# A new order of all engine and queue instructions in a sliding-window attention and MLP kernel

## The chip, the core and the metric

The kernel runs on one core of a Trainium2 chip. A core has five engines that work side by side, each with its own queue of instructions: PE (matrix products), DVE (elementwise work and reductions), ACT (activation functions and copies), POOL and SP (here almost only issuing of transfers). Every engine takes its instructions strictly in the order in which they were emitted, and an instruction that waits for another engine or for a transfer holds up all that stand behind it on its own engine. Transfers are carried out by 16 DMA engines; they are issued by POOL (transfers that change the type) and SP (stores and transposing transfers). The metric is the device time of one execution in microseconds (us), lower being better.

## The reference

q, k and v have 8 batches, 8 heads, 576 rows and 64 columns, all in 32 bits. Attention looks back over a window of 128 rows with a bias that falls linearly with distance; its output is laid out as 4,608 rows of 512, normalised, sent through a two-layer MLP with 2,048 hidden columns, and added back.

```python
scores = scale * np.matmul(q, k.transpose(0, 1, 3, 2))
rel = pos[:, None] - pos[None, :]
mask = (rel >= 0) & (rel < window)                      # window = 128
scores = np.where(mask, scores + bias[None], -1e9)      # bias = slope of the head * -|rel|
attn = np.exp(scores - np.max(scores, axis=-1, keepdims=True))
attn = attn / (np.sum(attn, axis=-1, keepdims=True) + 1e-09)
x = np.matmul(attn, v)                                  # then (8, 576, 512)
mu, var = mean(x), mean((x - mu) ** 2)                  # over the 512 columns
xn = (x - mu) / np.sqrt(var + 1e-06) * g_ln
out = x + np.maximum(xn @ w_ch1, 0.0) @ w_ch2           # 512 -> 2048 -> 512
```

## The kernel before

**Tiles.** The 4,608 rows are cut into 36 blocks of 128, numbered 0 to 35 in the order in which they are worked on. The blocks go through the MLP in 11 chunks: four of two blocks, then seven of four. Chunks 0 to 3 do the two products plainly; from chunk 4 (`SEVEN`) on the second product is done with seven instead of eight partial products, from chunk 8 (`BOTH`) on the first as well.

**The steps of a block i**, with the names that stand in the order and in the texts:

- `q`, `k`, `v`: loads that change 32 bits to 16 on the way, issued by POOL (L501). Blocks 0 and 1 are loaded uncast by SP instead (`qs`, `ks`, `v0`), and cast by ACT, DVE or POOL (`cT`, `cv`).
- `T` (PE transpose, L653 and L701) with its eviction `eT`/`ev` to the tile `qkt`; from block 9 on `QT`, a transposing transfer issued by SP (L716).
- `Z`: matmuls that put the bias into the scores' PSUM (L756; blocks 0 to 4). `S`: scores (L740). `exa`, `exb`: exponentials on ACT (L789), two halves. `mka`, `mkb`: masks on DVE (L797).
- `pva`, `pvb`: products with v, whose extra column gives the sums (L818). `rc`, `nm`: reciprocal and scaling on DVE (L835, L839).
- `mu`, `sq`, `ln`, `rs`, `xs`: the normalisation; `sq` (L866 on ACT, L868 on DVE) and `xs` (L878, L902 to L907) can be on either engine. `TX`/`xt`: transpose of the normalised block on PE with its eviction; from block 6 on `XT`, a transposing transfer by SP (L936).
- MLP: `A` first product (L1227) and `r` its relu (L1242 DVE, L1244 ACT); `B` second product (L1264) and `o` (L1272). In the seven-product form `Pa` to `Pg` (L1009) with `sa` to `sd`, `ra` to `rg` (L1021), and `Ua` to `Ug` (L1138) with `ca`, `ja`, `rja` and the like for the first product. `out`: stores by SP (L1081).
- `G`, `Gk`, `Gc`, `Gkc`: the normalisation's gain is spread over partitions once (L431, L445 on PE). `scaleW`, `sumW`, `sumT`: sums and scalings of weights for the seven products. `~n`: n small matmuls without use, issued to fill a wait of PE (L1305).
- `w`: the weights' loads (four of w1, four of w2), on POOL as well.

**Buffers that make a step wait.** `qk16` has 5 tiles (q and k of block n wait until block n-5 has been transposed, by `T` or `QT`), `vx` has 9, `qkt` 6 (`QT` of a block waits for the scores that read the tile last), `ot` (the tile that is stored) 3 and `xb` 4. POOL's loads take eight semaphores in turn, so a load also waits until the load eight places ahead of it has landed.

**What sets the order.** Every engine's order, the engine where there is a choice, and the PSUM bank are written out in the string `ORDER` (L119 to L212): words `name:engine`, where T is PE, A is ACT, V is DVE, G is POOL and S is SP, with the bank behind it; `.i` marks the issue of a transfer. `Plan.run` (L80 to L115) walks through the string, checks that each step's inputs and bank are there, and emits the steps in that order. The prices that `add` and `Choice` are given at build time play no part in it:

```python
def Choice(names, full):
    return dict(full)
...
            name, where = word.split(":")
            t, e, b = by[name].pop(0), self.ENGINES[where[0]], [int(x) for x in where[1:]]
            assert e in t.eng and all(ready(d) for d in t.deps), name
```

Of the kernel before, what the change touches and what calls it, by code (L numbers as in the profile page):

```python
# [127 lines left out]
A1.6:T1 r1.8:A ln1:A S4:T0 r1.6:A B1.0:T2 exb4:A k7.i:G A1.2:T3 B0.0:T0 r1.2:A pvb4:T1 B1.4:T2 q9.i:G mreg11:A rc1.4:V nm1.4:V exa4:A A1.12:T3
mreg31:A q8.i:G mreg10:A mreg01:A sumT0.0:V B0.4:T0 ln0:A r1.12:V rs0:A mreg00:A T5:T1 mreg30:A sumT0.1:V B0.8:T0 ev5:A v10.i:G sumT0.2:V B1.8:T2
mreg20:A k8.i:G mreg21:A S5:T0 mmixc:V B1.12:T2 exa5:A k9.i:G sumT1.0:V B0.12:T0 z1:V exb5:A k10.i:G sumT1.1:V o1.0:V B3.0:T3 dist1a:G q10.i:G o0.0:V  # L130
T6:T1 pva4:T2 B3.4:T3 ev6:V k11.i:G z2:V mka5:V S6:T0 v6.i:G B3.8:T3 exb6:A rc0.4:V mkb5:V q11.i:G T7:T0 nm0.4:V pva5:T1 mu4:V ev7:A k12.i:G B3.12:T3
xs4:V rc0.5:V rs1:A v7.i:G B2.0:T2 exa6:A nm0.5:V o3.0:V TX4:T0 q12.i:G sq4:A pvb5:T1 QT9.i:S sumT0.3:V T8:T3 xt4:A B2.4:T2 rc1.5:V k13.i:G nm1.5:V
ev8:A mkb6:V S7:T0 v8.i:G QT10.i:S B2.8:T2 mu5:V exa7:A mka6:V v8.i:G xs5:V exb7:A B2.12:T2 v9.i:G TX5:T0 mkb7:V S8:T0 xt5:A q13.i:G pva6:T1 o2.0:V
exb8:A pvb6:T3 A2.0:T0 v11.i:G rc0.6:V mka7:V A2.12:T2 nm0.6:V rc1.6:V QT11.i:S nm1.6:V A2.2:T1 r2.12:A mkb8:V r2.0:A A2.6:T3 mnewc:V exa8:A r2.2:V
pvb7:T2 pva7:T0 sq5:A mu6:V rc1.7:V r2.6:V S9:T0 QT12.i:S mka8:V A2.14:T1 exa9:A rc0.7:V nm1.7:V B4.0:T3 exb9:A nm0.7:V r2.14:V A2.4:T2 mu7:V xs6:V
S10:T0 q15.i:G r2.4:A xs7:V A2.10:T0 XT6.i:S exa10:A q15.i:G z3:V pva8:T1 mka9:V r2.10:A B4.4:T3 XT7.i:S k14.i:G exb10:A pvb8:T2 k15.i:G A2.8:T0
rc1.8:V rc0.8:V nm0.8:V q14.i:G S11:T0 nm1.8:V r2.8:A B5.0:T1 mkb9:V exb11:A mkb10:V QT13.i:S pva9:T2 B5.4:T1 ln2:A mka10:V exa11:A rc0.9:V pvb9:T0
k17.i:G B5.8:T1 rs2:A sq6:A rc1.9:V nm0.9:V mka11:V q16.i:G pva10:T2 sq7:A S12:T0 nm1.9:V B4.8:T3 v13.i:G exb12:A mu8:V mu9:V sq8:V B5.12:T1 k15.i:G
sq9:A rc0.10:V mkb11:V B4.12:T3 v12.i:G o5.0:V ln9:A rs9:A exa12:A A3.2:T0 xs8:V q17.i:G nm0.10:V XT8.i:S A3.0:T1 mka12:V r3.2:A k16.i:G xs9:A o4.0:V
A3.6:T2 QT14.i:S scaleW0:V r3.0:A pvb10:T0 pva11:T3 r3.6:A A3.14:T1 out1.0.i:S rc1.10:V S13:T0 nm1.10:V r3.14:A pvb11:T2 mu10:V exb13:A A3.10:T0  # L140
rc0.11:V rc1.11:V nm0.11:V nm1.11:V A3.4:T1 exa13:A sq10:V XT9.i:S B6.0:T3 r3.10:A mu11:V sq11:V r3.4:A out0.0.i:S A3.8:T2 mkb12:V ln11:A B7.0:T0
rs11:A xs10:A xs11:V B6.4:T3 scaleW1:V r3.8:A XT11.i:S ln3:A B7.4:T0 scaleW2:A XT10.i:S A3.12:T1 mka13:V mkb13:V pva13:T2 QT15.i:S k19.i:G B6.8:T3
r3.12:V scaleW3:A rc0.13:V sumT1.2:V S14:T0 q18.i:G pva12:T1 B7.8:T0 rc0.12:V v15.i:G QT16.i:S nm0.12:V B6.12:T3 nm0.13:V v17.i:G rs3:A exb14:A
pvb13:T1 pvb12:T2 k18.i:G exa14:A rc1.13:V B7.12:T0 o6.0:V QT17.i:S v14.i:G nm1.13:V A4.0:T3 sumT1.3:V v16.i:G A4.5:T1 rc1.12:V o7.0:V r4.0:A v15.i:G
mu13:V A4.8:T3 nm1.12:V sq13:A mu12:V q19.i:G mkb14:V out2.0.i:S S15:T0 r4.5:A A4.15:T0 out3.0.i:S exa15:A out5.0.i:S A4.6:T2 r4.15:V exb15:A mka14:V
A4.11:T1 sq12:V S16:T0 A4.1:T0 r4.11:V exa16:A r4.8:V A4.2:T1 exb16:A r4.1:V A4.3:T3 mka15:V r4.2:A QT18.i:S q22.i:G ln13:A mkb16:V A4.10:T0 r4.6:A
mkb15:V q20.i:G A4.9:T1 r4.10:A mka16:V rs13:A k20.i:G pva14:T2 r4.9:A A4.12:T0 rc0.14:V xs12:V r4.3:A k21.i:G pvb14:T1 XT12.i:S sa4.0:V S17:T0
v22.i:G A4.4:T3 exa17:A nm0.14:V out7.0.i:S rc1.14:V sc4.0:V q22.i:G A4.14:T2 r4.12:A nm1.14:V exb17:A q21.i:G mka17:V A4.13:T0 r4.4:A mkb17:V A4.7:T1
QT19.i:S r4.14:A r4.13:V pva15:T3 r4.7:A Pa4.00:T2 sb4.0:V out4.0.i:S xs13:A pvb15:T0 Pa4.01:T2 rc0.15:V rc1.15:V nm0.15:V Pb4.00:T1 nm1.15:V XT13.i:S
Pa4.10:T2 Pb4.01:T1 mu15:V sa4.1:V sq15:A Pa4.11:T2 mu14:V Pb4.10:T1 ra4.0:V sq14:A pva17:T3 Pb4.11:T1 sb4.1:V Pc4.00:T2 ln15:A rb4.0:V S18:T0 rs15:A  # L150
xs15:A Pc4.01:T2 xs14:V Pd4.00:T1 sc4.1:V XT14.i:S exb18:A Pc4.10:T2 rc0.17:V Pd4.01:T1 sd4.0:V exa18:A Pc4.11:T2 XT15.i:S nm0.17:V pva16:T0 rc4.0:V
Pd4.10:T1 pvb16:T3 sd4.1:V QT20.i:S Pd4.11:T1 q24.i:G S19:T0 Pe4.00:T2 rd4.0:V exb19:A k22.i:G Pe4.10:T2 mka18:V Pe4.01:T2 QT21.i:S exa19:A k22.i:G
rc0.16:V Pf4.00:T1 rc1.16:V nm0.16:V Pe4.11:T2 v19.i:G Pf4.10:T1 re4.0:V pvb17:T0 Pf4.11:T1 k24.i:G rc1.17:V nm1.16:V Pf4.01:T1 nm1.17:V Pg4.00:T2
v18.i:G mu16:V A5.13:T3 rf4.0:V sq16:A q23.i:G mu17:V mkb18:V A5.8:T0 sq17:A r5.13:V k23.i:G S20:T0 ln17:A A5.1:T1 v21.i:G A5.2:T3 r5.1:A v22.i:G
exa20:A A5.11:T1 v20.i:G r5.2:A Pg4.01:T2 mka20:V exb20:A Pg4.10:T2 r5.11:V QT24.i:S A5.3:T3 rs17:A r5.8:A mkb20:V k26.i:G pvb18:T1 Pg4.11:T2 r5.3:V
QT22.i:S q26.i:G S21:T0 rc1.18:V pva18:T0 nm1.18:V A5.5:T3 q25.i:G exa21:A rg4.0:V A5.0:T1 r5.5:V k25.i:G exb21:A xs16:V A5.10:T2 rc0.18:V mka19:V
A5.7:T3 r5.10:A mkb21:V A5.14:T2 r5.0:V r5.7:A mka21:V out9.0.i:S A5.6:T1 r5.14:A XT16.i:S mkb19:V xs17:A A5.9:T3 nm0.18:V r5.6:V out6.0.i:S pvb19:T2
pva19:T0 r5.9:V A5.12:T1 rc0.19:V mu18:V rc1.19:V QT23.i:S sq18:V A5.4:T3 r5.12:A nm1.19:V A5.15:T1 r5.4:A sa5.0:V Pa5.00:T2 nm0.19:V r5.15:A pvb20:T3
sc5.0:V XT17.i:S Pa5.01:T2 mu19:V Pb5.00:T0 rc1.20:V sq19:A nm1.20:V Pa5.10:T2 out8.0.i:S sb5.0:V pvb21:T1 out10.0.i:S Pb5.01:T0 ln19:A sa5.1:V
Pa5.11:T2 rs19:A QT25.i:S Pb5.10:T0 ra5.0:V xs19:A S22:T0 Pb5.11:T0 xs18:V exb22:A sb5.1:V Pc5.10:T2 XT19.i:S Pc5.00:T2 rb5.0:V exa22:A pva20:T3  # L160
Pc5.11:T2 XT18.i:S q28.i:G Pc5.01:T2 Pd5.00:T0 rc5.0:V k29.i:G S23:T0 QT26.i:S Pd5.01:T0 rc1.21:V exa23:A sd5.0:V k27.i:G Pe5.00:T2 sc5.1:V Pd5.10:T0
exb23:A v24.i:G Pe5.10:T2 nm1.21:V Pd5.11:T0 mkb22:V q29.i:G S24:T0 rd5.0:V Pe5.11:T2 q27.i:G Pe5.01:T2 rc0.20:V nm0.20:V Pf5.10:T0 sd5.1:V Pf5.00:T0
re5.0:V pva21:T1 dist1b:G v23.i:G A6.6:T3 mka22:V Pf5.11:T0 rc0.21:V dist2:G r6.6:A nm0.21:V Pf5.01:T0 k30.i:G exa24:A pva22:T3 mu21:V mkb23:V
# [1184 lines left out]
```

## Time and profile before

| | us |
|---|---|
| three runs | 299.85, 296.86, 299.59 |
| their median | 299.59 |
| the profiled execution | 299.22 |
| its span (first to last instruction) | 297.06 |
| outside the span | 2.16 |

TensorE's granted clock in the profiled execution is 0.998 of full speed. Times in a profile are counted from the span's start. Per cent behind an engine are its busy time over the span. PE is the matmuls, PEld the loading of their weights, which goes on beside them; the matmuls overlap one another, so a matmul's own duration is longer than the step from one start to the next. In a timeline a line is a run of like instructions: start, duration, engine, line of the kernel, operation, out<-in, shape, count, and in brackets the idle time before it with what ended it. In the chain of waits a line is start, duration and the work that the end of the program was waiting for at that moment.

| engine | busiest groups by line (busy us) |
|---|---|
| PE | A 89.9, P 45.5 and 30.5, B 31.2, pv 26.8 |
| ACT | exp 67.8, relu 37.7, sq 20.3, c* 19.5 |
| DVE | masks 30.1, nm 29.2, j* 23.9, relu 21.0, r* of P 19.6 |
| POOL | loads of q 32.6, k 32.8, v 30.7 (issuing) |

The queue of cast loads moves 17.70 MB and takes 91.8% of the span's DMA time as the packets' durations add up, the other transfers 21.77 MB and 42.5%. From issue to landing a cast load takes a median of 7.6 to 8.6 us, `QT` 8.7, `XT` 5.2, a store of 256 KB 3.5.

### The profile page before, as it was taken

What the parts mean: (1) busy time and instruction counts of PE and PEld (TensorE: products, weight loads), DVE (VectorE), ACT (ScalarE), POOL (GpSimd) and SP (SyncE); (2) the same over time, 40 slices, a digit from 0 to 9 for tenths busy, and PEclk for the clock granted to TensorE, in tenths of its full rate; (3) what the DMA queues carried; (4) which work ended last, traced back from release to release, by engine and by line L of the source; (5) the groups of instructions that cost most, each with busy time, mean ns of one, the idle gap of its engine ahead of it and who ended that gap; (6) DMA issues with size and microseconds to landing.
All of it is one profiled execution on the core that took longest, in us unless ns stands there. A gap on an engine that the chain in (4) does not pass through costs nothing.

```text
span 297.1 us, 8787 instructions
## 1 busy us (share of the span) xinstructions
PE 288.4 (97%) x3589; PEld 226.6 (76%) x3589; DVE 234.8 (79%) x623; ACT 201.1 (68%) x363; POOL 106.1 (36%) x139
## 2 busy tenths in 40 slices
PE   8889999999999999999999999799999999999995
...
GB/s 181 163 196 187 202 166 154 149 136 138 137 195 159 205 167 151 154 148 195 150 154 178 174 176 132 143 157 134 50 55 125 2 18 73 90 28 81 71 21 195
DMA packets 163787, 40.04 MB, mean 135 GB/s; under 512 B 154017, under 2 KB 159137, under 8 KB 163746
## 3 DMA queue, kind: packets, MB, share of 16 engines
q0 software_dynamic: 110000, 17.70, 91.8%
q1 hardware_dynamic: 53744, 21.77, 42.5%
...
q14 instruction: 13, 0.11, 0.1%
q10 hardware_dynamic: 2, 0.00, 0.0%
...
## 4 chain that ended last, share of the span: by engine, by line
PE 79%; DMA 15%; POOL 2%; issue 1%; SPq 1%; DVE 1%; POOLq 0%
PE fb L1009 25%; PE fb L1227 22%; PE u L1138 12%; PE fb L1264 10%; DMA vx<-in_v_dram 9%; PE fb L818 4%; PE sc L740 4%; DMA qkt<-qk 3%; DMA qk<-in_q_dram 2%; DMA ks<-in_k_dram 2%; POOL qk L501 1%; PE fb L701 1%; SPq L485 0%; PE fb L921 0%; PE sc L756 0%
## 5 line engine op out<-in xcount | busy, mean ns | idle before, releaser
L1227 PE MATMUL fb<-xt,w1sb 128*128 128x256 f16 (+1 forms) x512 | 89.9, 326 | 0.1
L789 ACT ACTIVATE probs<-sc 128x1024 f16<-128x1024 f32 (+1 forms) x72 | 67.8, 974 | 24.5 <-PE sc L740 18.4
L1227 PEld LDWEIGHTS <-w1sb 128*128 128x128 f16 x512 | 54.9, 114 | 24.7 <-issue 0.7
L1009 PEld LDWEIGHTS <-ht 128*128 128x128 f16 x560 | 53.1, 98 | 7.2
L1244 ACT ACTIVATE ht<-fb 128x512 f16<-128x512 f32 x65 | 37.7, 599 | 24.1 <-PE fb L1227 24.0
L501 POOL DMA_DIRECT2D qk<-in_q_dram x38 | 32.6, 862 | 49.1 <-DMA qkt<-qk 46.2
L1009 PE MATMUL fb<-w2sb,ht 128*128 128x256 f16 x336 | 45.5, 273 | 0.0
L501 POOL DMA_DIRECT2D qk<-in_k_dram x38 | 32.8, 870 | 25.4 <-DMA qkt<-qk 17.3
L797 DVE TENSOR_TENSOR probs<-probs,mreg 128x1024 f16<-128x1024 f16 (+1 forms) x46 | 30.1, 669 | 4.7 <-ACT probs L789 4.6
L501 POOL DMA_DIRECT2D vx<-in_v_dram x36 | 30.7, 867 | 6.2 <-DMA w2sb<-in_moe_w_ch_dram 1.5
L1264 PE MATMUL fb<-w2sb,ht 128*128 128x512 f16 x128 | 31.2, 379 | 0.0
L1009 PE MATMUL fb<-ks,ht 128*128 128x256 f16 x224 | 30.5, 273 | 0.0
L839 DVE SCALAR_TENSOR_TENSOR xb<-fb,rec 128x256 f16<-128x256 f32 x72 | 29.2, 417 | 0.7
L818 PEld LDWEIGHTS <-probs 128*128 128x128 f16 x544 | 23.9, 97 | 7.3 <-issue 2.2
L818 PE MATMUL fb<-vx,probs 128*128 128x65 f16 x496 | 26.8, 193 | 1.9 <-DMA vx<-in_v_dram 1.9
L1161 DVE TENSOR_TENSOR ht<-u,probs 128x512 f16<-128x512 f32 x36 | 23.9, 686 | 4.9 <-PE u L1138 1.9
L835 DVE RECIPROCAL rec<-fb 128x4 f32<-128x4 f32 x72 | 12.2, 177 | 18.4 <-PE fb L818 16.9
L1242 DVE TENSOR_SCALAR ht<-fb 128x512 f16<-128x512 f32 x31 | 21.0, 686 | 6.8 <-PE fb L1227 6.6
L1151 ACT ACTIVATE probs<-u 128x512 f32<-128x512 f32 x35 | 19.5, 596 | 9.4 <-PE u L1138 6.1
L1021 DVE TENSOR_TENSOR ot<-fb,xb 128x512 f32<-128x512 f32 (+1 forms) x31 | 19.6, 636 | 6.1 <-PE fb L1009 5.6
L866 ACT ACTIVATE squares<-xb,mean 128x512 f16<-128x512 f16 x28 | 20.3, 723 | 3.1 <-DVE mean L857 2.8
L1138 PEld LDWEIGHTS <-w1sb 128*128 128x128 f16 x192 | 21.1, 114 | 0.4
(119 smaller groups left out, 440.7 us busy)
## 6 DMA issues: line engine op xcount, KB each, us to landing
...
w2sb<-in_moe_w_ch_dram POOLq DMA_DIRECT2D x4, 512.0 KB, 10.9
...
```

What stands on the lines that cost most here:

```text
L501: nc.gpsimd.dma_start(out=dst(p0, n), in_=src[b, :, s0 : s0 + n, :].rearrange("h p d -> p h d"))
L789: nc.scalar.activation(out=o, in_=n_, func=AF.Exp, scale=inv_sqrt_d)
L797: en.tensor_tensor(out=pv, in0=pv, in1=mask[:, 2 * half : 2 * half + 2, :, lo:], op=ALU.mult)
L818: nc.tensor.matmul(pp[:, hh * (D + 1) : hh * (D + 1) + D + 1], probs[i][:, bank, slot, side * P : side * P + P], vx[i if side else before] ...
L839: nc.vector.scalar_tensor_tensor(out=xb[c][:, j, 256 * half : 256 * half + 256].rearrange("p (h d) -> p h d", d=D), in0=pp[:, :, 0:D], sca ...
L1009: nc.tensor.matmul(o, lhs(f, p), rhs(f), start=first and f == 0 and (p == 0 or key[0] != key[p]), stop=f == F2 - 1, skip_group_check=True)
L1138: nc.tensor.matmul(late[bank][:, FOURTH * f : FOURTH * f + FOURTH], w, rhs[kb], start=first and f == kb == 0, stop=kb == 1, skip_group_che ...
L1161: nc.vector.tensor_tensor(out=o, in0=late[bank][:, :].rearrange("p (f c) -> p f c", f=2), in1=other.rearrange("p (f c) -> p f c", f=2), op ...
L1227: nc.tensor.matmul(fb[b][:, n_ * x : n_ * x + n_], w1f[f // CB][:, kb, (f + x) % CB, :], xt[c][:, kb, 0:n_], start=(kb == x == 0), stop=(k ...
L1242: nc.vector.tensor_scalar(out=o, in0=src, scalar1=0.0, scalar2=None, op0=ALU.max)
L1244: nc.scalar.activation(out=o, in_=src, func=AF.Relu)
L1264: nc.tensor.matmul(pm[:, 0 : c1 - c0], ht[c][:, f, j * P : j * P + P], w2sb[f // CB][:, f % CB, c0:c1], start=(f == 0), stop=(f == NFB - 1),)
```

## The change

`ORDER` is replaced as a whole; the steps, their number and what each computes stay. Four things differ: the order of the steps on each of PE, ACT, DVE, POOL and SP; the PSUM banks; the engine of some steps (`sq` on ACT 28 before and 26 after, `xs` on ACT 18 and 14, the relu of the seven-product form `rja`, `rjb`, `rjc` on ACT 19 and 24, `r` on ACT 65 and 66, `scaleW` on ACT 2 and 3, `ev` on ACT 4 and 2, one cast of block 1 from POOL to DVE); and the filling matmuls, 59 before and 72 after. Two prices at build time change as well. The whole diff replaces 93 lines of the string by 93; shown are the start, the place of `q11`, the late loads with the transposes `QT28` to `QT34`, and the prices. In the late part the words ending in `.i:G`, read from left to right, are POOL's queue.

```diff
--- before.py
+++ after.py
@@ the start, down to A0.2 @@
-iden1:G qs0.0.i:S dist:G ks0.0.i:S dist00:G dist01:G qs1.0.i:S iden2:G sid6:V ks1.0.i:S sid2:V iden3:V sid4:V sid5:V sid7:V v0.i:S sid0:V sid3:V
-sid1:V ~35 Za0:T0 cT0.00:A g.i:A cT0.10:G w0.i:G T0.0:T0 k2.i:G Zb0:T0 eT0.00:A cT0.01:A cT0.11:G ~7 Sa0:T0 eT0.01:A q2.i:G ~5 T0.1:T1 exa0:A cv0:A
-v1.i:G eT0.10:V ~2 Za1:T0 eT0.11:A Sa1:T0 k3.i:G Sb0:T0 G:T2 exb0:A q3.i:G Zb1:T0 Gc:A v3.i:G Sb1:T0 exa1:A pva0:T0 pvb0:T1 v2.i:G Gk:T2 rc0.0:V
-rc1.0:V exb1:A nm1.0:V nm0.0:V w1.i:G mu0:V w3.i:G xs0:V ~10 T2:T1 w2.i:G Z2:T0 ev2:V pva1:T0 q5.i:G pvb1:T3 rc0.1:V S2:T0 rc1.1:V nm0.1:V exb2:A
-k4.i:G nm1.1:V T3:T1 exa2:A mu1:V TX0:T0 q4.i:G xs1:V Z3:T0 xt0:A ev3:V v4.i:G pvb2:T3 TX1:T0 pva2:T1 S3:T0 xt1:V q8.i:G rc1.2:V exa3:A nm1.2:V
-A0.2:T0 w4.i:G rc0.2:V sq0:V exb3:A A0.6:T3 dist1:G Gkc:V nm0.2:V sq1:A A0.4:T2 r0.2:V k8.i:G mu2:V pvb3:T1 xs2:V r0.4:A pva3:T0 Z4:T0 sq2:A rc1.3:V
+dist:G qs0.0.i:S dist00:G ks0.0.i:S iden1:G dist01:G qs1.0.i:S iden2:G sid6:V v0.i:S sid3:V sid7:V sid5:V sid2:V sid4:V sid1:V ks1.0.i:S sid0:V
+iden3:V ~31 Za0:T0 Zb0:T0 cT0.00:A g.i:A cT0.10:G v1.i:G T0.0:T0 cT0.01:A w3.i:G eT0.00:A q2.i:G ~10 Sa0:T0 G:T1 exa0:A k2.i:G cT0.11:V cv0:A eT0.01:A
+k3.i:G T0.1:T2 Za1:T0 eT0.10:V v2.i:G Sa1:T0 eT0.11:A Sb0:T0 exb0:A q3.i:G exa1:A ~8 Zb1:T0 w0.i:G pvb0:T0 pva0:T2 Sb1:T0 rc1.0:V rc0.0:V k4.i:G
+nm1.0:V exb1:A nm0.0:V q4.i:G mu0:V Gc:A ~13 pvb1:T0 pva1:T2 xs0:V v3.i:G rc0.1:V w2.i:G ~10 T2:T3 k5.i:G TX0:T1 ev2:V Z2:T0 rc1.1:V q5.i:G nm1.1:V
+S2:T0 Gk:T3 exb2:A nm0.1:V w1.i:G exa2:A mu1:V xs1:V T3:T0 xt0:A v4.i:G sq0:V sq1:A TX1:T2 Z3:T0 xt1:V w4.i:G ev3:V pvb2:T1 pva2:T2 rc1.2:V w5.i:G
+rc0.2:V S3:T0 nm0.2:V A0.2:T0 exb3:A nm1.2:V q6.i:G T4:T2 exa3:A A0.12:T1 ev4:V r0.2:A mu2:V Z4:T0 r0.12:V pvb3:T2 k8.i:G A0.0:T0 rc1.3:V xs2:V k6.i:G
@@ the words around q11 (middle) @@
...
+v5.i:G A1.0:T2 r0.14:V mmixc:V B0.0:T0 r1.0:A mnewc:V B1.0:T1 mkb5:V r1.4:V B0.4:T0 z3:V A1.6:T2 T6:T3 sumT0.0:V B1.4:T1 ev6:A q11.i:G mka5:V B0.8:T0
+rs0:A k9.i:G sumT0.1:V rs1:A S6:T0 z2:V r1.6:V k10.i:G B1.8:T1 exa6:A q10.i:G A1.14:T3 exb6:A B0.12:T0 q8.i:G r1.14:A k11.i:G pva4:T2 B2.0:T3 o0.0:V
+rc0.4:V k8.i:G B1.12:T1 nm0.4:V mka6:V v6.i:G T7:T0 o1.0:V B2.4:T3 v7.i:G pva5:T2 B2.8:T3 q12.i:G rc0.5:V QT9.i:S mu4:V nm0.5:V sq4:A B3.0:T1 xs4:V
...
@@ the late loads and transposes @@
...
-QT28.i:S A6.7:T0 q32.i:G sa6.0:V mkb25:V sq23:A A6.15:T1 q30.i:G mkb26:V out12.0.i:S r6.4:A A6.14:T2 k32.i:G r6.7:V r6.15:A sb6.0:V A6.13:T3 r6.14:A
-v26.i:G sc6.0:V ln23:A Pa6.00:T0 rs23:A r6.13:V dist2a:G Pb6.00:T1 xs23:A q31.i:G pvb24:T2 Pa6.01:T0 rc1.24:V xs22:A k31.i:G sa6.1:V XT23.i:S
-Pb6.01:T1 Pa6.10:T0 nm1.24:V k31.i:G pva25:T3 sb6.1:V XT22.i:S Pa6.11:T0 k34.i:G Pb6.10:T1 ra6.0:V S27:T0 pvb25:T2 q33.i:G rc0.25:V sc6.1:V Pb6.11:T1
-QT30.i:S Pc6.00:T0 nm0.25:V k33.i:G Pc6.10:T0 rb6.0:V pva24:T3 Pc6.11:T0 q34.i:G exa27:A rc0.24:V rc1.25:V Pd6.00:T1 nm1.25:V exb27:A Pc6.01:T0
-v28.i:G mka26:V Pd6.01:T1 rc6.0:V S28:T0 v29.i:G pvb26:T2 exa28:A nm0.24:V Pd6.10:T1 mu25:V v31.i:G rc1.26:V pva26:T3 sd6.1:V Pd6.11:T1 exb28:A
-Pe6.00:T0 sd6.0:V v30.i:G QT31.i:S Pe6.10:T0 nm1.26:V Pe6.01:T0 v31.i:G rc0.26:V rd6.0:V S29:T0 Pe6.11:T0 exb29:A nm0.26:V A7.3:T2 QT32.i:S re6.0:V
-v35.i:G exa29:A A7.8:T3 mka27:V v34.i:G mu24:V mkb28:V sq24:A Pf6.10:T1 mkb29:V Pg6.00:T0 r7.3:A v33.i:G Pg6.10:T0 mu26:V mka28:V r7.8:A Pf6.00:T1
-sq25:A mkb27:V Pg6.01:T0 sq26:V Pg6.11:T0 k35.i:G ln25:A S30:T0 rg6.0:V pvb27:T2 pva27:T3 Pf6.11:T1 rc1.27:V exb30:A rc0.27:V out18.0.i:S mka29:V
-Pf6.01:T1 A7.15:T0 v32.i:G nm1.27:V exa30:A nm0.27:V A7.0:T2 rf6.0:V rs25:A r7.15:A q35.i:G mu27:V pvb28:T3 xs24:V r7.0:A pva28:T1 QT33.i:S rc1.28:V
-S31:T0 rc0.28:V mka30:V pva29:T0 exa31:A A7.11:T2 nm1.28:V QT34.i:S rc0.29:V exb31:A nm0.28:V A7.1:T3 mka31:V r7.11:A A7.4:T1 mkb31:V r7.1:V pvb29:T2
...
+exb25:A A6.3:T3 mka25:V r6.4:A A6.12:T1 XT20.i:S r6.3:V q32.i:G A6.15:T0 sa6.0:V r6.12:A r6.7:A mkb25:V out12.0.i:S Pa6.00:T3 k31.i:G r6.15:A
+Pb6.00:T1 sb6.0:V k32.i:G Pa6.01:T3 QT29.i:S sa6.1:V Pb6.01:T1 mu22:V Pa6.10:T3 v27.i:G sc6.1:V sq22:A Pb6.10:T1 sb6.1:V Pa6.11:T3 v28.i:G pvb24:T2
+ra6.0:V Pb6.11:T1 QT30.i:S dist2a:G S27:T0 rc1.24:V pva24:T0 rb6.0:V Pc6.10:T3 exb27:A rc0.24:V Pc6.00:T3 sd6.1:V ln23:A Pd6.00:T1 rs23:A nm0.24:V
+Pc6.11:T3 xs23:A sc6.0:V Pd6.01:T1 nm1.24:V pva25:T0 Pc6.01:T3 exa27:A xs22:V Pd6.10:T1 rc6.0:V XT22.i:S pvb25:T2 Pd6.11:T1 sd6.0:V S28:T0 XT23.i:S
+Pe6.00:T3 mu24:V rc1.25:V exa28:A rd6.0:V Pe6.10:T3 rc0.25:V Pe6.01:T3 nm1.25:V exb28:A k34.i:G QT31.i:S Pe6.11:T3 nm0.25:V pvb26:T2 sq24:A re6.0:V
+Pf6.10:T1 q33.i:G pva26:T0 rc1.26:V S29:T0 mka28:V v31.i:G Pf6.00:T1 exa29:A mkb28:V QT32.i:S Pf6.11:T1 v29.i:G nm1.26:V Pg6.10:T3 exb29:A rc0.26:V
+Pf6.01:T1 mkb27:V v34.i:G mka27:V Pg6.11:T3 nm0.26:V Pg6.00:T3 k33.i:G mu25:V pva27:T2 rf6.0:V S30:T0 sq25:A pvb27:T0 Pg6.01:T3 k35.i:G rc1.27:V
+exa30:A rc0.27:V A7.8:T1 nm1.27:V rg6.0:V v31.i:G A7.7:T0 r7.8:A mka30:V q35.i:G exb30:A A7.11:T3 nm0.27:V mkb29:V v30.i:G r7.7:A pvb28:T1 r7.11:V
+pva28:T2 S31:T0 q34.i:G rc0.28:V A7.13:T0 rc1.28:V mu26:V exb31:A mka29:V v32.i:G nm0.28:V A7.10:T3 exa31:A nm1.28:V v33.i:G A7.9:T2 mu28:V r7.13:A
+mkb31:V ln25:A v35.i:G pva29:T1 mka31:V r7.9:A pvb29:T0 S32:T0 rc0.29:V r7.10:A QT33.i:S sumW1.0:V A7.2:T2 exa32:A nm0.29:V dist1a:G dist1b:G rc1.29:V
+A7.4:T3 sumW0.0:V r7.2:A nm1.29:V rs25:A sq26:A A7.1:T1 mu27:V xs25:V mka32:V A7.0:T2 exb32:A xs24:V A7.3:T0 r7.4:A mkb32:V XT24.i:S r7.0:A A7.15:T3
+mkb30:V r7.1:A out14.0.i:S sumW0.1:V r7.3:A A7.6:T2 out15.0.i:S r7.15:A sa7.0:V sq27:A A7.12:T1 sumW0.2:V QT34.i:S pva30:T0 r7.6:A sc7.0:V A7.5:T3
+ln27:A rc0.30:V r7.12:A sumW1.1:V A7.14:T2 r7.5:A nm0.30:V rs27:A sb7.0:V pva31:T1 r7.14:A QT35.i:S Pa7.00:T3 rc0.31:V sq28:A pvb30:T0 nm0.31:V S33:T0
...
@@ the two price lines @@
-        ag = add(f"sq{i}", Choice("ACT DVE", {"ACT": 0.94, "DVE": 0.86}), e_sq, [mu], stats_v)
+        ag = add(f"sq{i}", Choice("ACT DVE", {"ACT": 1.01, "DVE": 0.82}), e_sq, [mu], stats_v)
...
-                xs_ = add(f"xs{x}", Choice("DVE ACT", {"DVE": 0.5, "ACT": 1.0}), e_xs, [rs], av(x, 6.6))
+                xs_ = add(f"xs{x}", Choice("DVE ACT", {"DVE": 0.48, "ACT": 1.24}), e_xs, [rs], av(x, 6.6))
```

More of the change, by code (lines that the diff above doesn't have):

```diff
@@ L128 @@
[L128 to L163, printed above, removed]
```

112 lines of the change are left out of this document (71 added, 41 removed).

## The prediction

> **What bounds the kernel now.** First the page: busy shares, then the slices.
>
> ```profile
> span 297.1 us, 8787 instructions
> PE 288.4 (97%) x3589; PEld 226.6 (76%) x3589; DVE 234.8 (79%) x623; ACT 201.1 (68%) x363; POOL 106.1 (36%) x139
> ...
> PE   8889999999999999999999999799999999999995
> ```
>
> PE is the resource, and it misses full slices only at the start (below 22 us) and in one slice near 190 us. The order gives PE the same matmuls before and after, so only the start, the late hole and the tail behind the last matmul (3.7 us, its stores) can change. From the matmul groups I took start-to-start times where nothing waited (four 512-column matmuls 0.865 us, four 256-column ones 0.437, scores 0.47, pv 0.24) and added up the PE work that is left behind each instruction. Start plus work left is 285.9 at A0.2 (19.26), the first MLP product, 286.2 at 26 to 33 us, 289.5 at 178, and 292.8 to 293.2 from 208 to the end. The rise up to 178 is mostly the 0.095 us in front of each scores group, in both orders. The rise from 178 to 208 is the hole. PE's timeline shows its three stops:
>
> ```profile
> 187.85 0.19 PE L818 MATMUL fb<-vx,probs 128*128 128x65 f16 x1
> 188.93 0.61 PE L818 MATMUL fb<-vx,probs 128*128 128x65 f16 x15 [0.88 <-DMA vx<-in_v_dram]
> ...
> 189.94 0.20 PE L818 MATMUL fb<-vx,probs 128*128 128x65 f16 x1
> 190.92 0.37 PE L818 MATMUL fb<-vx,probs 128*128 128x65 f16 x7 [0.78 <-DMA vx<-in_v_dram]
> ...
> 204.53 0.19 PE L818 MATMUL fb<-vx,probs 128*128 128x65 f16 x1
> 205.00 0.37 PE L818 MATMUL fb<-vx,probs 128*128 128x65 f16 x7 [0.28 <-DMA vx<-in_v_dram]
> ```
>
> Start to start these are 1.08, 0.98 and 0.47 instead of 0.03 each: **2.4 us**, for v28, v29 and v32. The chain of waits says why they were late:
>
> ```profile
> 165.79 8.79 DMA qkt<-qk
> 174.58 0.02 issue
> ...
> 177.74 0.87 POOL vx L501
> 178.60 12.28 DMA vx<-in_v_dram
> 190.88 0.28 issue
> 191.16 13.79 DMA vx<-in_v_dram
> 204.96 0.04 issue
> 205.00 0.37 PE fb L818 x7
> ```
>
> POOL issued no load from 169.4 to 175.12: q33 stood first in its queue and waited until QT28, the transpose that reads q33's buffer, had landed (174.58). Fourteen loads then went out together and landed between 182.07 and 205.77, each far slower than the 0.87 us apart of loads near 150 us. v32 could be issued only when v29 had landed: eight loads are outstanding at most.
>
> **The change part by part.** The two price lines feed a dictionary of which only the keys are read, so they emit nothing. The new ORDER is the change. The profiled execution is 299.22, its span 297.06, and 299.22 is 0.37 under the median of the runs.
>
> *Engines.* sq moves 2 from ACT to DVE, xs 4 from ACT to DVE, the rja/rjb/rjc group 5 from DVE to ACT, scaleW 1 to ACT, two evictions and one cast to DVE. By the groups' means (ACT sq 0.72, DVE sq 0.74, ACT xs some 1.0, DVE xs 0.4 to 0.75) this is about -1.8 us on ACT and +1.6 on DVE. With 68% and 79% busy neither sets the pace behind 26 us: 0. Were the cover gone in one place, it would cost one operation, 0.7 us.
>
> *Start.* The same 26 PE tasks lie ahead of A0.2, and the same work behind it, so its start moves the end one for one. Before:
>
> ```profile
> 13.91 0.62 PE L701 MATMUL fb<-iden,qk 128*128 128x128 f16 x8 [0.65 <-DMA qk<-in_q_dram]
> ...
> 16.60 0.62 PE L701 MATMUL fb<-iden,qk 128*128 128x128 f16 x8 [0.79 <-DMA qk<-in_q_dram]
> ...
> 19.26 2.41 PE L1227 MATMUL fb<-xt,w1sb 128*128 128x256 f16 x20
> ```
>
> T2 and T3 wait for loads, and S3 goes straight into A0.2. In the new order ACT casts qs1 (landed 6.53, 0.77) ahead of eT0.00 (0.60): 7.90. Sa0 ends at 8.2, and behind it stand G (0.96) and T0.1 (0.75): 9.9. Then ACT has eT0.01 and eT0.11 (0.6 each, 11.15), exb0 0.6, exa1 and exb1 0.97 each: 13.7. pvb1/pva1 need exb1, and with ten warm matmuls (0.56) behind them T2 starts at 14.85. T2 0.45 and ev2 0.69 lead to S2 at 16.0, S2 takes 0.34, and Gk (0.89), which stood in idle time at 11.65, now stands between S2 and T3: T3 at 17.3. DVE has rc, nm, nm, mu, xs1 to 17.85, then sq0 (0.74, moved ahead), xt1 (0.43) and ev3 (0.69): 19.7. S3 0.47 gives A0.2 at 20.2: **+1.0**. Lower bound 0.0, if ACT's early operations fit and the loads alone count (T2 at 13.9); upper +2.0, if k2 and q3 land last in their spans (15.2 and 17.8, two places of 0.87 later each). Weights w0, w2, w1 come at about 19.5, 23.8 and 28.0 (2.4 to 2.5 apart); A0.6 needs w1 at 27.9: 0, at most 0.5. The 13 more warm matmuls fill waits.
>
> *Middle.* q11 now stands ahead of k9, k10, q10, k11, v6 and the halves of block 8, and it waits for T6 at about 40 us. v6 then lands at 51.6 to 53.5 for pva6 at 55.4: 0, and about 2 us of margin that would be lost first. SP's order changes little: out14 and out15 move behind XT24, 9 us of PE work ahead of ra7.0, which waits for their buffer; they take 3.5 us by the median and at most 7.75: 0.
>
> *Late.* v28 is issued directly behind v27 and ahead of the load that now blocks the queue, k34, and lands about ten us before its use: its stop goes, and with it the reason of v29's and v32's, as the queue stands: **-2.4**. In exchange there is a new burst behind QT29: k34 q33 v31h v29 v34 k33 k35 v31h q35 v30 q34 v32 v33 v35. QT29 stands where 120.4 us of work is left, near 170; with 8.8 us and the 0.5 to issue the burst starts at 179.2. I lay the old burst's landings on it, place by place, counted from the first issue at 175.12. Fourth place +13.8: v29 at 193.0, due at 191.8. Sixth place +16.3: k33 at 195.5, and QT33 (8.7 to 10.9 in the burst) at 204.2 or later. S33 stood at 203.61; without the stops ahead of it (2.0) and with the start (+1.0) it is due at 202.6: +1.6. Eleventh place +27.2, less what one transpose fewer in flight gives back (3.2, QT35's time alone): q34 at 203.2, QT34 3.2 to 8.7 later, 206.4 to 211.9, and S34 is due 4.4 behind S33, at 207.0: -0.6 to +4.9. These don't add up, since a later wait finds what an earlier one has taken; the middle of the last, **+2.1**, holds the others. Bounds: 0, if the loads come at the mean of the old burst (2.36 per load, k33 at 192.2) with QT34 alone; +8.1, if the eleventh place is +27.2 whole and QT34 takes 8.7.
>
> *Sum.* 297.06 + 1.0 - 2.4 + 2.1 = 297.8, +0.7 against the profiled execution, so 299.59 + 0.7: **300.3**.
>
> **The rivals.** (a) *Slower: S33 and S34 come late in full.* k33 was second in the old burst and is sixth, q34 was third and is eleventh. For it: QT31 to QT34 took 8.8 to 12.1 us there. Against it: with k33 later, one or two transposes less compete with the loads. With +8.1 it is 306.3; from +4.4 on it is slower by over 1%: 0.31.
>
> (b) *Faster: no late stop and a free start.* 299.59 - 2.4 - 1.2 (what small waits are in the rise up to 178) = 296.0. For it: A0.2's cost hangs on seven ACT operations that might fit. Against it: Gk and sq0 stand on the path whatever the loads do, 1.6 us: 0.14.
>
> (c) *PE has headroom in its weight loads.* Groups of four 256-column matmuls take 0.437 us, their loads 4 x 0.098 = 0.39; if an order could bring 196 such groups down to the loads' time, that is 0.047 x 196 = 9.2 us, 290.4. Against it: the last 30 groups run without a wait, 13.12 us, 0.437 each, so no order closes that: 0.03. The Trainium skill, "Perfetto Trace Analysis", section "Identifying the Most-Contended Engine", holds that PE's matmul busy share is a bad measure of headroom and that the share of its weight loads is the better one: 76% here, against 97%. By that rule the trace would leave room that the waitless stretch doesn't show.
>
> (d) *The change does nothing measurable*, start and hole trading places: this is the forecast's own neighbourhood.
>
> **How the numbers follow.** 1% is 3.0 us, about the spread of the three runs (296.86 to 299.85) and what can be told from no change. The forecast's case (start +1, late stops moved rather than removed, 297 to 302.6) has 0.52; (a) 0.31, (b) 0.14, (c) 0.03. So faster by over 1% (below 296.6) 0.17, within 0.52, slower (above 302.6) 0.31. The range leaves out (c), the best of (b) and the last fifth of (a): 296.0 to 305.0.
>
> **What would show it.** The first L1227 matmul at 20.2 (start right) or near 19.3 (wrong). No wait of L818 for a v load at 187 to 189. A wait of L740 on DMA qkt<-qk, or of PE in front of it, between 200 and 215: its length is the late term. Start plus work left then rises there and nowhere else. The prediction is wrong if PE stops in the middle for v6, or if L1021 waits for a store, or if ACT or DVE holds PE behind 26 us.

## The result and the profile after

The changed kernel takes 300.36 us (median of 17 runs, 298.35 to 303.52), the kernel before 298.14 beside it on the same chip (17 runs, 296.66 to 299.85). The ratio is 1.0057, with a 95% interval of 1.0033 to 1.0080: slower by 1.7 us. Executions more than 1.5% above their kernel's fastest count in no ratio and no table, here three of the changed kernel's 17 (the other fourteen have a median of 299.91) and the one that was profiled in its first repeat (303.90). The forecast was 300.3 and "within 1%". The profiled execution took 300.15, with a span of 298.3.

The page of the changed kernel answers the lines of before:

```profile
span 298.3 us, 8809 instructions
...
PE 289.0 (97%) x3602; PEld 228.1 (76%) x3602; DVE 237.6 (80%) x624; ACT 197.9 (66%) x359; POOL 105.5 (35%) x138
...
PE   7889999989999999999999999999999999999995
```

PE is as busy as before. The late hole is gone from the slices (the one 7 among the nines, before); the start is a tenth lower, and there is a new 8 in the ninth slice, near 66 us. PE's timeline, v28 and v29 in the late part, start and duration in us, has no brackets any more:

```profile
190.75 0.65 PE L818 MATMUL fb<-vx,probs 128*128 128x65 f16 x16
191.80 2.78 PE L1227 MATMUL fb<-xt,w1sb 128*128 128x512 f16 x12
194.41 0.65 PE L818 MATMUL fb<-vx,probs 128*128 128x65 f16 x16
```

Each block's sixteen products are now one piece. In place of these stops PE waits at the start, in the same view:

```profile
14.56 0.40 PE L701 MATMUL fb<-iden,qk 128*128 128x128 f16 x4 [0.38 <-DMA qk<-in_q_dram]
15.45 0.40 PE L701 MATMUL fb<-iden,qk 128*128 128x128 f16 x4 [0.49 <-DMA qk<-in_k_dram]
20.65 1.06 PE L1227 MATMUL fb<-xt,w1sb 128*128 128x256 f16 x8
22.17 0.62 PE L701 MATMUL fb<-iden,qk 128*128 128x128 f16 x8 [0.45 <-DMA qk<-in_q_dram]
...
27.25 0.62 PE L701 MATMUL fb<-iden,qk 128*128 128x128 f16 x8 [0.22 <-DVE xs L878]
...
29.81 0.95 PE L1227 MATMUL fb<-xt,w1sb 128*128 128x256 f16 x7 [0.27 <-DMA w1sb<-in_moe_w_ch_dram]
```

T2, T4 and A0.6 stand behind loads (T5 too: q5 landed at 27.21). Three quarters of the chain of waits from 5 to 31 us are two weights (start, duration, what):

```profile
5.43 0.96 POOL vxp L501
6.39 7.26 DMA w1sb<-in_moe_w_ch_dram
13.65 0.28 issue
...
18.25 11.52 DMA w1sb<-in_moe_w_ch_dram
29.77 0.05 issue
```

The first of them is w3, issued behind v1. Its landing lets out the load eight places behind it, q4, and the last of the fifteen loads that PE needs by then, w1, lands at 29.77.

The prediction's measure, start plus PE work left, shows where the two differ. The kernels of the runs below are in it too; every row is one profiled execution, us:

| | A0.2 | T6 | S27 | end of PE |
|---|---|---|---|---|
| before | 285.9 | 286.5 | 289.4 | 293.4 |
| before, second profile | 286.3 | 286.7 | 290.4 | 291.7 |
| changed | 287.3 | 289.2 | 293.4 | 294.6 |
| changed, third run | 287.7 | 289.7 | 292.3 | 293.5 |
| changed, w3 ahead of v1 | 286.6 | 288.7 | 291.6 | 292.7 |
| before, v1 ahead of w0 | 289.0 | 289.4 | 293.6 | 294.9 |

From the start to T6 (near 41 to 45 us) the change loses 2.5 to 3.2; from T6 to the end the new order rises by 3.8 to 5.4 and the old one by 5.0 to 6.9. With two profiles of each that is 4.6 and 6.0 in the mean, so the new order wins back about 1.4; single pairs run from -0.4 to 3.1. In the last row the start holds a stretch at half the clock as well (below).

### The profile page after: what moved, and what is told of

Read it like the earlier page. It is cut to its first block, busy times and chain, and to the rows that moved or that the text cites. A ratio compares the mean times of both kernels' runs of the same rounds, so it can differ in the third digit from the quotient of the medians.

```text
span 298.3 us, 8809 instructions
## 1 busy us (share of the span) xinstructions
PE 289.0 (97%) x3602; PEld 228.1 (76%) x3602; DVE 237.6 (80%) x624; ACT 197.9 (66%) x359; POOL 105.5 (35%) x138
## 4 chain that ended last, share of the span: by engine, by line
PE 84%; DMA 9%; POOL 2%; DVE 2%; SPq 1%; issue 1%; DVEq 0%
PE fb L1009 29%; PE fb L1227 26%; PE u L1138 12%; PE fb L1264 7%; DMA w1sb<-in_moe_w_ch_dram 6%; PE fb L818 5%; PE sc L740 4%; DMA out_dram<-ot 2%; DMA ks<-in_k_dram 1%; POOL qk L501 1%; POOL vxp L501 1%; SPq L936 1%; PE fb L701 0%; DVE ot L1021 0%; DVE ht L1242 0%
## 5 line engine op out<-in xcount | busy, mean ns | idle before, releaser
L1227 PE MATMUL fb<-xt,w1sb 128*128 128x256 f16 (+1 forms) x512 | 88.6, 327 | 0.4 <-DMA w1sb<-in_moe_w_ch_dram 0.3
L1227 PEld LDWEIGHTS <-w1sb 128*128 128x128 f16 x512 | 55.2, 114 | 25.5 <-issue 0.4
L1009 PE MATMUL fb<-w2sb,ht 128*128 128x256 f16 x336 | 44.1, 273 | 0.0
L1009 PE MATMUL fb<-ks,ht 128*128 128x256 f16 x224 | 29.8, 273 | 0.0
L1242 DVE TENSOR_SCALAR ht<-fb 128x512 f16<-128x512 f32 x30 | 20.4, 684 | 7.3 <-PE fb L1227 6.8
L1151 ACT ACTIVATE probs<-u 128x512 f32<-128x512 f32 x35 | 19.9, 599 | 8.8 <-PE u L1138 8.6
L1021 DVE TENSOR_TENSOR ot<-fb,xb 128x512 f32<-128x512 f32 (+1 forms) x31 | 19.5, 635 | 5.1 <-PE fb L1009 5.0
L866 ACT ACTIVATE squares<-xb,mean 128x512 f16<-128x512 f16 x26 | 18.7, 720 | 5.4 <-DVE mean L857 5.4
```

The lines of the kernel that those rows point to most:

```text
L1009: nc.tensor.matmul(o, lhs(f, p), rhs(f), start=first and f == 0 and (p == 0 or key[0] != key[p]), stop=f == F2 - 1, skip_group_check=True)
L1227: nc.tensor.matmul(fb[b][:, n_ * x : n_ * x + n_], w1f[f // CB][:, kb, (f + x) % CB, :], xt[c][:, kb, 0:n_], start=(kb == x == 0), stop=(k ...
L1242: nc.vector.tensor_scalar(out=o, in0=src, scalar1=0.0, scalar2=None, op0=ALU.max)
```

## The experiments

Ratios are to the kernel before, run on the same chip in the same hours, with 95% intervals. The times are medians of all executions. The labels are shortened to e1 to e12: e1 to e4 shared a chip, so did e5 to e8, e9 and e10, and e11 and e12. The edits are moves of words in `ORDER`. Waits in e2, e3, e8 and e10 are counted start to start, 0.07 to 0.17 above the idle time that a view gives; elsewhere they are that idle time.

**The changed kernel again** (no edit), once beside the mixed orders and once, as `e11_after_third`, beside the last run.

> The changed kernel unaltered, to see which of its waits come again. In its first profile, start plus work left stood above the kernel before by 1.4 us at A0.2, 2.7 at T6, 3.7 at S14, 4.0 at S27 and 1.2 at the end. Theory: the loads at the start are a fixed sequence, so +1.4 at A0.2 and +2.7 at T6 come again within 0.3, and no stop stands behind 175 us. Open: the 1.03 us inside the scores of block 10 that nothing in the profile explains; if it is part of the order it comes again at that place, if it is chance it does not, and the span is some 1 us shorter, 297.3 instead of 298.3.

300.16 us, 1.0039 (0.9998 to 1.0079). Its profile is the one left out above, so the question went to the next repeat:

> The changed kernel unaltered beside the next run on one chip. Theory (v1 ahead of w3 costs the start and makes it uneven): ratio to before 1.004 to 1.008, executions from 298.4 up to 301 or more, where the kernel with w3 first had 298.0 to 299.4 in 12. Rival (the run with w3 first fell on a good chip): median below 299.3.

300.78 us (299.14 to 304.31), 1.0101 (1.0070 to 1.0131). The start came again, with 287.7 and 289.7 in the table 0.4 and 0.5 above the first profile, where 0.3 was expected. The 1.03 us inside the scores of block 10 did not: S10 to S11 rose by 0.13 instead of 1.35. It is chance, not part of the order, and no stop stood behind 175 us.

**Old start, new rest, and the reverse (e2, e3).** The words of one order up to and with S6, then those of the other that are left; PSUM banks that clash at the seam are set anew.

```diff
-<after: words up to S6>  <after: the rest>
+<before: words up to S6> <after: the words that are left>      # e2
-<before: words up to S6> <before: the rest>
+<after: words up to S6>  <before: the words that are left>     # e3
```

> The order of before up to and with S6 (near 45 us), then the new order. Theory (start and late part add up): the new start's 2.7 us go and nothing comes in their place, so 300.4 - 2.7 = 297.7, 0.4 under the kernel before at its median of 298.1; 296.7 if the 1.03 us wait in block 10 does not come either. Rival (the late start is slack that the late loads need): PE comes to v29, S33 and S34 2.7 us sooner, these have margins of 4.3, 2.8 and 4.5 us in the first profile, and stops of 1 us or more appear there: 298.7 to 300.4.

300.15 us, 1.0066 (1.0026 to 1.0106): no gain. The profile has two waits that the changed kernel lacks, one made by the seam (S7, 1.03, for an eviction on DVE) and one in the middle, 1.69 for XT19 at A6.11; there its margin in the changed kernel was 0.75. Its start was not quite the old one either: behind a stop of 1.30 for q2 the granted clock was 0.50 from 16 to 18 us, and T6 stands at 287.6, 0.8 to 1.1 above the other profiles with the old start. The run decides nothing between the two readings, and was made again as e10.

> The new order up to and with S6, then the order of before. Theory: 2.7 us on top of before, 300.8, with the three stops of before at v28, v29 and v32 as they were. Rival (the stops take up what the start lost, because the late loads are bound by the transfers and not by PE): the stops shrink from 2.4 us to about 0 and the time is 298.4.

300.24 us, 1.0072 (1.0029 to 1.0114). The time lies between the two figures, 1.5 to 2 above before. The late stops did not come: v28 landed at 188.1 for use at 192.0, v29 at 192.5 for 193.0. Instead S16 waited 1.10 and S20 0.91 for QT transposes. The theory has most of the size, since other waits came in the middle. That a PE 3 to 4 us later finds v28 and v29 landed fits the rival, but isn't shown to be the reason: a second profile of the kernel before (e8, below) has no late stop either, with PE only 0.8 us later than in the first.

**v28 and v29 ahead of the blocked load, in the kernel before (e4).**

```diff
-... k34.i:G ... q33.i:G ... k33.i:G ... q34.i:G ... v28.i:G ... v29.i:G
+... k34.i:G ... v28.i:G v29.i:G q33.i:G ... k33.i:G ... q34.i:G
```

> The kernel before with v28 and v29 issued ahead of q33, which waits for QT28, and nothing else moved. Theory (the blocked queue made v28, v29 and v32 late): v28 and v29 land before 181 us, all three stops go, 298.1 - 2.4 = 295.7. Rival (the stop moves to what stands next): k33 and q34 land no earlier than before, S33 and S34 or v30 and v31 wait instead, and 1 us or more comes back: 296.7 to 298.1.

298.98 us, 1.0036 (0.9987 to 1.0084): no gain. v28 landed at 181.7 and v29 at 183.4, for use at 189.4 and 190.5, and no stop for a load is in the late part; PE ends at 292.6. That the blocked queue made them late holds. That this costs a usual execution 2.4 us does not, as the next run shows.

**The kernel before, a second profile (e8).**

> The kernel before unaltered, for a second profile. Theory (the late stops are its own, whatever came earlier): stops of 2 us or more at v28, v29 and v32 again. Rival (they are what is left over when PE comes through the middle without a wait; in the mixed order with the new start the same late orders had none): this run has waits of 0.5 us or more in the middle, and the late stops are smaller by about as much; the end of PE is then within 1 us of the first profile's 293.4.

297.59 us in the profiled execution, PE ends at 291.7. Its timeline at v28 and v29:

```profile
188.65 0.65 PE L818 MATMUL fb<-vx,probs 128*128 128x65 f16 x16
189.70 0.42 PE L818 MATMUL fb<-vx,probs 128*128 128x65 f16 x8
```

No stop. v28 had 3.1 us to spare here and v29 0.9, where in the first profile they were about 1 us late; one wait of 0.74 in the middle (at 142.7) is all it had behind the start. So the theory fails, and the rival in part: it put the end of PE within 1 us of 293.4. The first profile, at 299.22, had caught an execution 1.1 us above the median of 298.14.

**The head of the late burst as before** (e5, in the changed kernel).

```diff
-k34.i:G q33.i:G v31.i:G v29.i:G v34.i:G k33.i:G ... q34.i:G ...   QT33.i:S XT24.i:S out14.0.i:S out15.0.i:S QT34.i:S
+k34.i:G q33.i:G k33.i:G q34.i:G v31.i:G v29.i:G v34.i:G ...       QT33.i:S QT34.i:S XT24.i:S out14.0.i:S out15.0.i:S
```

> The changed kernel with the late burst's head put as in the kernel before: k34 q33 k33 q34 and then v31h v29 and the rest, and QT34 issued directly behind QT33. Theory (loads are slow while several transposes are in flight, so the place in the burst alone does not set a landing): QT33 and QT34 go out 4 to 8 us sooner, beside QT31 and QT32, and the loads behind them land late as they did before: v29 at 193 or later instead of 190.1, v30 and v32 3 us or more later than in the changed kernel (196.3 and 199.0), and the time is 300.4 to 302, with a stop at v29 if PE is early. Rival (places alone): v29 two places later, at 191.8, v30 at 196 and v32 at 199 as they were, the time is 300.4.

301.69 us in four runs (298.34 to 304.0), 1.0137 (1.0075 to 1.0200) by three of them. The profiled execution was the fastest of them; its burst began 1.0 us sooner than the changed kernel's. QT33 went out at 188.8 instead of 193.3 and QT34 at 190.2 instead of 201.1. v29 landed at 192.3 (0.2 before its use) instead of 190.1, v30 at 200.3 instead of 196.3, v32 at 201.5 instead of 199.0. Counted from the burst's first issue these are 3.2, 5.1 and 3.4 later; at the 0.87 at which loads land alone, the loads that now stand ahead and did not before make up 1.7 of the first, 0.9 of the second and nothing of the third. The theory's mechanism holds: the transposes that the early k33 and q34 let out slow the loads behind. No stop came in that execution, with 0.2 us left at v29 and v30; that other executions lose more there is likely, but not shown.

**T4 and T5 later, and w3 later** (e6 and e7, in the changed kernel; the second has both). The evictions, scores and exponentials of the two blocks move along where they must, and two or three PSUM banks change.

```diff
-A0.2 T4 A0.12 ... TX2 T5 A0.8 S5 TX3 A0.6 A1.2 A1.8       w2.i:G k5.i:G q5.i:G w1.i:G
+A0.2 A0.12 T4 ... TX2 A0.8 TX3 A0.6 A1.2 T5 A1.8 S5       w2.i:G w1.i:G k5.i:G q5.i:G      # e6
-v1.i:G w3.i:G q2.i:G k2.i:G k3.i:G v2.i:G q3.i:G w0.i:G
+v1.i:G q2.i:G k2.i:G k3.i:G v2.i:G q3.i:G w0.i:G w3.i:G                                     # e7, and T4 behind pvb3
```

> The changed kernel with three things set later at the start: T4 behind A0.12, the loads k5 and q5 behind w1, and T5 with its eviction and scores behind A1.2. Theory (of the 1.75 us between A0.2 and A0.6 the waits for q4, q5 and w1 are 1.5): start plus work left stays within 0.5 of its value at A0.2 up to T6, the three waits go, 300.4 - 1.4 = 299.0. Rival (transfers bound the first 200 us, so PE's gain turns into waits for transposes in the middle): the line at T6 is 1.5 lower, but at S27 less than 0.5 lower than the changed kernel's, and the time is 300 to 300.5.

> As the run before, and the load of w3 moved from second place to behind w0, so that q2, k2, k3, q3 and w0 land about 2.4 us sooner. Theory: T2 and T3 then wait for ACT's chain (exb1, the eviction) and not for q2 and q3, A0.2 is at 19.9 instead of 20.6, and the time is 300.4 - 2.1 = 298.3, about that of the kernel before. Rival (transfers bound): 300 to 300.5 as in the run before.

301.54 us, 1.0106 (1.0060 to 1.0151), and 302.59, 1.0139 (1.0099 to 1.0179): both slower, against theory and rival. In the first A0.2 came only at 21.98, through nothing that was moved: PE had stood 1.90 for an eviction of block 0, and the granted clock was 0.58 and 0.57 from 8 to 12 us. In the second A0.2 did start at 19.57, as expected, and the line stood at 286.2 there; by T6 it was 291.8. The waits for q4, q5 and w1 had given way to waits that the moves had made: A0.8 1.42 behind a relu that now stood behind two exponentials on ACT, A1.8 0.78 behind the eviction of block 5, 1.09 for v3; two waits for weights, 0.32 and 0.55, were left. They leave open whether T4 and T5 could be moved at no cost.

**w3 ahead of v1** (e9, in the changed kernel, nothing else).

```diff
-v1.i:G T0.0:T0 cT0.01:A w3.i:G eT0.00:A q2.i:G
+w3.i:G v1.i:G T0.0:T0 cT0.01:A eT0.00:A q2.i:G
```

> The changed kernel with the load of w3 issued ahead of v1 instead of behind it, nothing else. In the first 30 us of every run so far the loads land one after the other, so what the queue loses early every later load lacks; in the new start the transfers ran at 84 and 100 GB/s from 7 to 9 us, in the old one at 109 and 201, and the old one begins with a weight. Theory (transfers bound the start): q2, q3 and w1 land 0.6 to 1.0 us sooner (14.5, 17.9 and 29.8 in the first profile), A0.2 and the line at T6 come down as much, 300.4 - 0.8 = 299.6. Rival (PE's and ACT's own order bounds the start): these loads land sooner, T2 and A0.6 do not follow, 300.4.

298.80 us (12 runs, 297.98 to 299.43), 0.9999 (0.9973 to 1.0025): no loss is left in the ratio. The changed kernel was not run beside it; its own three ratios are 1.0057, 1.0039 and 1.0101. Part of the level comes from the other side: 9 of the 23 executions of the kernel before beside it have a granted clock of 0.994 or less, none of these 12, and among those at 0.997 or more the means are 298.76 and 298.28. q2 landed at 13.13 instead of 14.51, q3 at 17.43 instead of 17.88, w1 at 29.29 instead of 29.77 (against the third run of the changed kernel 1.8, 0.9 and 1.0 sooner). The line is 0.7 lower at A0.2 and 0.5 at T6, and the waits behind T6 that the changed kernel's first profile had did not come. But e3 and e5 have the changed kernel's start too, with v1 first, and there q2 landed at 13.33 and 13.98, w1 at 29.45 and 29.19, and T6 stands near 288.9 and 288.6, hardly above the 288.7 with w3 first or below it. So the profiles don't show that w3's place lowers the line at T6; what speaks for it is the ratio.

**The converse, in the kernel before (e12).**

```diff
-w0.i:G k2.i:G q2.i:G v1.i:G k3.i:G
+v1.i:G w0.i:G k2.i:G q2.i:G k3.i:G
```

> The converse: the kernel before with the load of v1 issued ahead of w0 (fourth place before), nothing else. w0, k2 and q2 stand one place later, so by the order alone T2 comes 0.9 us later, and every load behind them lands when it did: k3 15.8 to 16.1, w2 25.4 to 25.7. Theory (a load of 128 KB at the head loses time of the queue that a weight at the head does not): the loads behind land 0.5 to 1.0 us later as well, w2 at 26 to 26.6, and the time is 1.0 to 1.6 above the kernel before. Rival (order alone): w2 as before, A0.2 0.5 to 0.9 later, the time 0 to 0.9 above.

300.47 us (298.70 to 303.95), 1.0074 (1.0044 to 1.0104): the old order loses about what the changed one had lost. k3 landed at 17.04 and w2 at 27.00, where five profiles with the old start have 15.75 to 16.40 and 25.42 to 25.97. So loads whose place hasn't changed come 0.6 to 1.3 and 1.0 to 1.6 us later too, the theory's 0.5 to 1.0 or more. A0.2 came at 22.39, later than either reading allows. PE had stood for 2.20 us in front of T2, for q2, and behind that the granted clock fell; the page has it in the third slice, where the kernel before has a 9:

```profile
PEclk9979999999999999999999999999999999999999
```

It was 0.60 from 16 to 18 us and 0.54 from 18 to 20, which by these figures cost PE about 1.7 us (an estimate). So 289.0 in the table is the later loads and the clock together. Seven of the nine executions have a granted clock of 0.994 or less, 8 of 18 of the kernel before beside them; how much of the 0.7% is the stream alone isn't shown.

The windows by time show when the queue falls behind (window, its length, busy us of the engines, then the granted clock, DMA share and GB/s). First the kernel before, and the same with v1 first:

```profile
7.00:8.00 1.00, 0.90 (x15) 0.48 (x7) 0.00 (x0) 1.00 (x3) 0.57 (x2) 1.00 0.98 109
8.00:9.00 1.00, 0.73 (x8) 0.67 (x8) 0.26 (x1) 0.93 (x2) 1.00 (x3) 1.00 1.23 201
9.00:10.00 1.00, 1.00 (x28) 0.62 (x26) 0.17 (x1) 0.84 (x3) 1.00 (x2) 1.00 1.25 200
```

```profile
7.00:8.00 1.00, 1.00 (x15) 0.58 (x15) 0.00 (x0) 1.00 (x3) 1.00 (x2) 1.00 1.33 95
8.00:9.00 1.00, 0.12 (x2) 0.06 (x2) 0.00 (x0) 1.00 (x3) 1.00 (x3) 1.00 1.28 71
9.00:10.00 1.00, 1.00 (x20) 0.76 (x24) 0.42 (x1) 0.14 (x2) 1.00 (x2) 1.00 0.98 163
```

Then the changed kernel, and the same with w3 first:

```profile
8.00:9.00 1.00, 1.00 (x8) 0.67 (x7) 0.33 (x1) 1.00 (x3) 1.00 (x3) 1.00 1.36 100
9.00:10.00 1.00, 1.00 (x33) 0.69 (x31) 0.42 (x1) 0.67 (x2) 1.00 (x2) 1.00 1.18 185
```

```profile
8.00:9.00 1.00, 1.00 (x4) 0.47 (x5) 0.46 (x1) 0.98 (x2) 1.00 (x2) 1.00 1.11 182
9.00:10.00 1.00, 1.00 (x24) 0.76 (x25) 0.42 (x1) 0.67 (x3) 1.00 (x2) 1.00 1.25 204
```

In the six profiles with a weight first the transfers are at 150 to 208 GB/s from 8 to 9 us; in six with v1 first (the changed kernel's two, e3, e5, e6 and e12) they move 62 to 123 in that microsecond and 163 or more in the next. The weight was issued one place (0.96 us) later, and v1 alone is slow: the queue of cast loads moved 429 to 838 packets from 7 to 8 us in these six, and 1,217 from 13 to 14 us in the kernel before, where 128 KB loads follow one another. (The DMA share adds up the packets' durations over the engines' time; above 1 it doesn't say how much was moved.) The Trainium skill, "DMA: Bandwidth & Descriptors", section "Anatomy of one DMA — SWDGE (gpsimd) path", puts a fixed 2.0 us on each such transfer, with half of full efficiency only at some 860 KB. By the formula that the Trainium skill gives there v1 would land 2.3 us after its issue, an estimate. In these six profiles it took 3.4 to 4.2, and no row separates a fixed part.

**Old start, new rest, without the seam's wait (e10).**

```diff
-T7:T1 ... ev7:V
+T7:T1 ev7:A                # in the mixed order of e2
```

> The old start with the new rest once more, with one wait of the seam removed: the eviction of block 7 is on ACT directly behind T7, where DVE had it 2 us late and S7 waited 1.0 us, pva6 0.45 more. Theory (start and rest add up, the seam hid it): the line at T6 is near 287.0 as in the other old starts, it rises by 4 to 5.4 us to the end as in the other new rests, PE ends at 291 to 292.4 and the time is 297.5, below the kernel before by 0.5 to 1. Rival (transfers bound the middle, so a PE that is 2 us ahead waits for them): waits of 1 to 2 us for QT or XT transposes between 90 and 190 us, 299 to 300.

299.63 us (296.96 to 300.87), 1.0013 (0.9977 to 1.0049). S7's wait is gone, T6 stands at 286.8 as expected, and the rest then rises by 7.1 to 293.9: 0.85 in B5.8, in front of pva11, for nothing that the profile shows, 0.82 at A4.11 behind an output tile that waited for its store, 0.63 for XT19. Only the last is a transpose. In this profile the new rest doesn't keep its lead behind a PE that comes 2 us sooner, so its gain and the old start's don't add up here. For the median that is likely and not shown: the interval reaches down to 0.9977, into the theory's 0.5 to 1 us below the kernel before.

No version beat both kernels by more than its interval. The changed kernel with w3 first is level with the one before; against the changed kernel it was not run on one chip.

## Why the prediction came out right

The sum was right for the profiled pair (+0.7 forecast; 300.15 against 299.22 is +0.9) and two of its terms were not; they happened to cancel. By the table the changed kernel gains +1.4 up to A0.2, +1.3 from there to T6, +1.3 from T6 to S27 and -2.8 from S27 to the end of PE, where +1.0, 0, 0 and -0.3 were forecast. That 300.3 fell on the median is luck beyond that: it was built on 299.59, the median of the three runs on record, and with 17 runs the kernel before has 298.14. The change cost 1.7 by the ratio (1.0 to 2.4 by its interval), not 0.7.

*Start, +1.0.* A0.2 came at 20.65, +1.4; in four other profiles of the new start that can be read it came at 20.07 to 21.98, in five of the old one at 19.26 to 20.61. The size is right, the place is only half right: T2 had ACT's chain (with w3 first it still starts at 14.43, though its loads had landed by 14.07), q2 (14.51) and, for its second half, k2 (15.40) at its back. T3 at 17.93 stood 0.96 behind Gk, which takes 0.89, so Gk's new place held it as forecast, and q3 (17.88) would have held it as long. What the head of POOL's queue costs was in the upper bound, by two places of a load, and had no term. By the runs' times it is the largest single cost found; the line at T6 doesn't show it, since two profiles with v1 first (e3 and e5) stand about as low there as the one with w3 first.

*A0.2 to A0.6, 0, at most 0.5.* The step that failed by its size. w1 was put at 28.0 and landed at 29.77; T4 waited for q4, T5 for q5, A0.6 for w1, 0.65, 0.39 and 0.44 on the line, where the old order had 0.28 in all. The weights were forecast at 19.5, 23.8 and 28.0 and came at 20.4, 25.5 and 29.8: the stream was 1 us late at w0 and 0.8 more by w2. The head of the queue is at most a part of it: with w3 first these weights came at 19.9, 25.0 and 29.3. T4 and T5, set ahead of where they were, were priced as PE work alone, without the four loads that they need.

*Middle, 0.* Right: v6 landed at 54.1 for use at 56.9, and L1021 waited for no store. The 1.03 us in block 10's scores had no place in it and did not come again.

*Late, -2.4.* The stops went, as forecast, with v28 landing at 178.2. But the same profile of before that showed them was taken for the kernel's habit. A second one has none, so the median gains less than 2.4 by it; how much is not settled, since two profiles can't give a frequency.

*Late, +2.1 for S33 and S34.* The step that failed outright. k33 landed at 193.3 (forecast 195.5), QT33 at 202.4, 3.0 before its use; q34 at 198.5 (203.2), QT34 at 205.3, 4.7 before. The old burst's landings, laid on the new one place by place, carried the old burst's transposes with them. The text's own remark against rival (a), that later k33 and q34 leave fewer transposes to compete, was what happened, and putting k33 and q34 first brought the late landings back. (Two readings in the working were loose: five of the old burst's thirteen steps from landing to landing are 0.53 to 0.90, so not each load was far slower than 0.87; and k33 at 2.36 per load would be 193.4, not 192.2, which leaves the lower bound at 0.)

*Rivals.* (a) did not occur, nor (b): the start cost its microsecond. The rival (c) stays as it was: from 210 us on PE runs without a wait in the changed kernel too.

What stays open: w3 first has the lower time, by 1.6 to 2 (298.8 against 300.2 to 300.8 in three sets of runs, on other chips), but its line at T6, 288.7, lies within the 288.6 to 289.7 of four profiles with v1 first. The difference may be waits further on that the looser start lets in, as in the first profile, or executions with a worse start. One of the latter is on record, in the first repeat: k2 landed at 17.02 instead of 15.40, PE stood for 1.97 us, the granted clock was then 0.50 from 17 to 25 us, and A0.2 came at 25.48. But of the changed kernel's 37 executions only 5 have a granted clock under 0.997, and without them its three medians are still 299.9 to 300.3. So this is not the whole of it, and the profiles taken don't tell the rest apart.
